# Staging the plain attention heads token by token through DRAM, with two direct batches and partial first sums

## The chip, the cores and the metric

The kernel runs on one core of one Trainium2 chip. The metric is the device time of one execution in microseconds (us), as the median of several runs. The hardware profiler also took one execution; its trace has the start and length of every instruction, and "the span" is the time from its first instruction to its last.

## The reference, cut to what matters

Eight batches of eight heads with 576 tokens and a head dimension of 64 go through windowed causal attention. Heads 0 to 3 ("plain") see the last 32 tokens; heads 4 to 7 ("dilated") see every fourth of the last 128. The result, 4608 tokens by 512, goes through an MLP with 2048 inner columns.

```python
mask_plain = (rel >= 0) & (rel < window)
mask_dil = (rel >= 0) & (rel < window * dilation) & (rel % dilation == 0)
...
x = np.ascontiguousarray(attn_out.transpose(0, 2, 1, 3)).reshape(B * S, H * D)
...
h = x @ w_in
g = h * (1.0 / (1.0 + np.exp(-beta * h)))
return (g @ w_out).astype(np.float32)
```

Inputs and output are fp32; the kernel multiplies in bf16 and sums in fp32 in PSUM.

## The kernel before

The MLP goes over nine tiles of 512 tokens. A tile has 16 h slots, one for each 128 of the 2048 inner columns, of four matmuls each (`slot_h`, L824: one for each k-tile of 128 of the 512 columns of x), and 16 o slots of four matmuls (`block`, `block_cols`, L856: four blocks of 128 tokens, four slots each). After an h slot ACT takes a tanh (L831) and DVE makes the gate (L836, g). After four o slots ACT or DVE scales the block into osb (L873, L875), and SP or ACT stores it (L881). The k-tiles 0 and 1 of x hold the plain heads, 2 and 3 the dilated ones. Of tile 0, the first four h slots are cut into 288 and 224 columns (SPLIT), since a batch's x comes in two halves of 288 tokens.

Attention of a batch is worked between the slots of the MLP, about two tiles ahead. Its steps have names in the lists FIRST (batches 0 to 2) and LATER (the rest). S2 and S3 are scores of dilated heads (L644), as pairs of matmuls on 64 rows each; T is the scores of the last 16 tokens of each dilated class (L618, from dkt and qt); S00 and so on are scores of the plain heads in blocks of 96 queries. ACT takes the exponential (L586), DVE or POOL multiplies by a mask (L590), V.. and U multiply by the values (L740, L725, L755), DVE normalizes (L604, L605) into xsp, xdm and xdt, and X.. brings the result into xT: by PE transposes in batches 0 and 1 (L778, L780, L796), by DRAM in the others (`back_dma`: writes x<-xsp, x<-xdm, x<-xdt on SP, then the crossbar, a transposing DMA, from DRAM to xT at L490).

K and Q come in two ways. Batches 0 to 2 (DIRECT) are loaded into st by `direct_qk` and transposed on TensorE (KD and QD for dilated heads, L427; KP and QP for plain ones, L434, as 64x64 pairs), then copied into dk, dq, kT and qT. Batches 3 to 7 are cast from fp32 to bf16 into DRAM (s) on POOL's DMA queue (`cast`, `load`, issued at L368), in rows of 1024 elements, and brought by four crossbars on SP (`crossbar`, L417) into dk and dq, and into raw for the plain heads. There, even and odd tokens lie on the two halves of the partitions, so `spread` copies them into kz, which is padded with zeros to 128 rows, and qd (L218, on DVE or POOL). The plain scores of these batches are matmuls over all 128 rows (L703, with masks maske), those of batches 0 to 2 pairs over 64 rows (L678, with masks maskn). A cast from batch 4 on waits for the crossbars of the batch before.

v is loaded three times by POOL's queue: vp (plain, 128-byte rows in bf16), vt (the tails), and vd16 or st, copied into vd. The late masks and the zeros of kz are made on POOL in one step, t_late (L317 to L362).

The order of all instructions on every engine is written out by a planner (`Plan`). Each step has engines with costs, dependencies and a due time vt, given in tiles. `run` takes, again and again, the step that can start first, and among those that can start at nearly the same time (NEAR) the one that is due first. PSUM is eight banks; CAPS says how many may be held for each kind of use. Where nothing is ready before 80 us of the plan, it puts in filler matmuls on zeros (L968). The engines then work strictly in this order, each waiting on semaphores. POOL issues the loads and casts (queue q0), SP the crossbars, write-backs and stores (queue q1).

Of the kernel before, what the change touches and what calls it, by code (L numbers as in the profile page):

```python
# [9 lines left out]
BF16 = mybir.dt.bfloat16  # L10
ACT = mybir.ActivationFunctionType
ALU = mybir.AluOpType
# [10 lines left out]
class Op:  # L23
    def __init__(self, engs, fn, deps, vt, acquire, group, dma, lat):
# [10 lines left out]
class Plan:  # L35
# [3 lines left out]
    CAPS = {"h": 3, "o": 2, "z": 4, "a": 8, "s": 5}  # L39
# [6 lines left out]
    def op(self, engs, fn, deps=(), vt=0.0, acquire=None, group=None, dma=0, lat=None):  # L46
        acquire = acquire if acquire is None or isinstance(acquire, list) else [acquire]
        o = Op(engs, fn, deps, vt, acquire, group or acquire, dma, lat)
        self.ops.append(o)
        return o  # L50

    def run(self, filler=None, filler_until=0.0):
# [13 lines left out]
        ends = []  # L66

# [19 lines left out]
        while n_left:  # L87
            best = None
            near = {}
            for o in avail:  # L90
                base = o.ready
                at = {e: max([free[e], base] + [t for x, t in o.group.read.items() if x != e]
                             if o.group is not None and e != "PE" else [free[e], base]) for e, d in o.engs}
                fin = min(at[e] + d for e, d in o.engs)
# [18 lines left out]
            if filler is not None and s <= filler_until and free["PE"] + 300 < s:  # L113
# [5 lines left out]
                free["PE"] = now + 225  # L119
                continue  # L120
# [6 lines left out]
            o.fn(e)  # L127
            free[e] = s + d
            o.start, o.end = s, s + d + self.LAT[e]
# [27 lines left out]
FIRST = "KD0 QD0 KD1 QD1 KP0 QP0 KP1 QP1 S2 S3 T S00 S10 V20 V21 V30 V31 U V00 V10 X2 X3 X00 X10 S01 S11 V01 V11 X01 X11"  # L157
LATER = "S2 S3 T V20 V21 V30 V31 U S00 S10 S01 S11 X2 X3 V00 V10 X00 X10 S02 S12 V01 V11 X01 X11"
# [3 lines left out]
def kernel(  # L162
# [34 lines left out]
    DIRECT = 3  # L197
    ADDED = 1
    BY_DMA = 2
    SPLIT = 4  # L200
# [16 lines left out]
    def copy(e, out, in_):  # L217
# [10 lines left out]
    mask_e = {n: const([P, 2, 2, 2, QT // 2], BF16, f"maske_{n}") for n in ("FP", "PP")}  # L228
# [14 lines left out]
    ptt = const([P, 2, 288], BF16, "ptt")  # L243
    ptt_own = ptt[0:2 * KTL][:, :, 0:256].rearrange(
        "p c (h s) -> p c h s", h=4)[:, :, :, 0:2 * UT]
# [9 lines left out]
    raw = const([P, 2, 4, S // 2], BF16, "raw")  # L255
    vd16 = raw[:].rearrange("p z h m -> p (z h m)")[:, 0:1024].rearrange("p (h T d) -> p h T d", h=4, T=C)
    vd16_of = [vd16] * DIRECT + [st[b % 2][:, 0:1024].rearrange(
        "p (h T d) -> p h T d", h=4, T=C) for b in range(DIRECT, B)]
    kT = [const([P, WIN + S], BF16, f"kT{x}") for x in range(2)]
    kz = const([P, 4, WIN + S], BF16, "kz")  # L260
    qd = const([P, 4, 2, S // 2], BF16, "qd")
    qT = qd[:].rearrange("p (x f) e m -> p x (f e m)", x=2)[:, :, 0:S]
# [27 lines left out]
    def t_fill1(e):  # L290
        for x in range(2):
            nc.vector.memset(kT[x][:, 0:WIN], 0.0)
# [709 lines left out]
```

The softmax here doesn't subtract the row's maximum and nothing guards it: scores larger than these inputs give would overflow.

## Time and profile before

| what | us |
|---|---|
| median of 3 runs | 311.29 (310.63 to 311.44) |
| the profiled execution | 311.41 |
| its span | 309.7 |
| TensorE busy (PE) | 297.0 |
| VectorE busy (DVE) | 199.1 |
| ScalarE busy (ACT) | 171.3 |
| GpSimd busy (POOL) | 108.6 |
| first h slot begins | 20.07 |

The granted TensorE clock was 0.998. PE is matmuls, PEld the loads of weights beside them. A line of the timeline has the start, the busy time, the engine, the line of the kernel, the operation, its output and input by their names, the tile and the count; in brackets stands the idle time before it and what ended that. Ends of matmuls are modelled, so a group's own cost is read from the start of the next. A digit in the slices is a share of busy time in tenths of one fortieth of the span.

### The profile page before, as it was taken

What the parts mean: (1) busy time and instruction counts of PE and PEld (TensorE: products, weight loads), DVE (VectorE), ACT (ScalarE), POOL (GpSimd) and SP (SyncE); (2) the same over time, 40 slices, a digit from 0 to 9 for tenths busy, and PEclk for the clock granted to TensorE, in tenths of its full rate; (3) what the DMA queues carried; (4) which work ended last, traced back from release to release, by engine and by line L of the source; (5) the groups of instructions that cost most, each with busy time, mean ns of one, the idle gap of its engine ahead of it and who ended that gap; (6) DMA issues with size and microseconds to landing.
All of it is one profiled execution on the core that took longest, in us unless ns stands there. A gap on an engine that the chain in (4) does not pass through costs nothing.

```text
span 309.7 us, 6029 instructions
## 1 busy us (share of the span) xinstructions
PE 297.0 (96%) x2270; PEld 153.6 (50%) x2307; DVE 199.1 (64%) x421; ACT 171.3 (55%) x302; POOL 108.6 (35%) x150
## 2 busy tenths in 40 slices
PE   7899999999999999999999999999999999999994
PEld 5565546454454445444455454445544444444452
DVE  4687868888958777775896878677853443434300
ACT  2668845866448445753775547555754544554311
POOL 8989754537170146414823651154000000000000
PEclk9999999999999999999999999999999999999999
DMA  6999999999689982999999759997024100001112
GB/s 100 168 210 207 206 187 208 230 155 174 155 163 178 191 151 83 180 160 181 188 206 181 197 117 177 129 224 163 18 64 112 44 34 34 36 34 60 42 70 69
DMA packets 93561, 42.48 MB, mean 137 GB/s; under 512 B 71052, under 2 KB 88220, under 8 KB 93212
## 3 DMA queue, kind: packets, MB, share of 16 engines
q0 software_dynamic: 42336, 19.66, 50.3%
q1 hardware_dynamic: 51052, 22.37, 35.0%
q8 instruction: 18, 0.29, 0.4%
q14 instruction: 11, 0.09, 0.1%
q10 hardware_dynamic: 144, 0.07, 0.1%
HBM read 39.32 MB, written 18.87 MB: 188 GB/s over the span
## 4 chain that ended last, share of the span: by engine, by line
PE 82%; POOL 6%; DMA 6%; DVE 2%; issue 2%; ACT 0%; POOLq 0%; ACTq 0%; DVEq 0%
PE bank L856 38%; PE bank L824 35%; DMA raw<-in_v_dram 3%; DMA vp<-in_v_dram 3%; PE bank L703 2%; PE bank L755 2%; POOL st L368 1%; PE bank L740 1%; PE bank L644 1%; PE bank L725 1%; POOL kz L362 1%; DVE qt L218 1%; DVE g L836 1%; PE bank L434 0%; PE bank L618 0%
## 5 line engine op out<-in xcount | busy, mean ns | idle before, releaser
L831 ACT ACTIVATE tnh<-bank,beta_half 128x512 bf16<-128x512 f32 (+2 forms) x148 | 100.1, 677 | 81.8 <-PE bank L824 73.6
L836 DVE SCALAR_TENSOR_TENSOR g<-tnh,bank 128x512 bf16<-128x512 bf16 (+2 forms) x148 | 98.7, 670 | 69.2 <-ACT tnh L831 68.1
L824 PE MATMUL bank<-xT,w_in_bf 128*128 128x512 bf16 (+2 forms) x576 | 139.8, 373 | 1.3 <-DVE xT L218 0.3
L856 PE MATMUL bank<-w_out_bf,g 128*128 128x512 bf16 (+1 forms) x571 | 137.7, 373 | 1.8 <-DVE g L836 0.5
L856 PEld LDWEIGHTS <-g 128*128 128x128 bf16 x592 | 55.4, 98 | 58.6 <-issue 0.8
L824 PEld LDWEIGHTS <-w_in_bf 128*128 128x128 bf16 x592 | 55.1, 98 | 58.2 <-issue 0.8
L873 ACT ACTIVATE osb<-bank 128x512 f32<-128x512 f32 (+2 forms) x36 | 21.0, 582 | 28.4 <-PE bank L856 23.5
L586 ACT ACTIVATE pt<-bank 128x384 bf16<-128x384 f32 (+1 forms) x54 | 22.0, 455 | 6.4 <-PE bank L703 3.5
L586 ACT ACTIVATE ptd<-bank 128x512 bf16<-128x512 f32 x32 | 17.0, 601 | 10.3 <-PE bank L644 10.3
L605 DVE TENSOR_TENSOR xsp<-bank,rcp 96x384 bf16<-96x384 f32 x32 | 17.7, 554 | 1.1
L604 DVE RECIPROCAL rcp<-bank 128x4 f32<-128x4 f32 (+2 forms) x72 | 12.8, 177 | 5.5 <-PE bank L755 2.8
L218 POOL COPY kz<-raw 64x1152 bf16<-64x1152 bf16 x6 | 9.4, 1566 | 18.4 <-DMA raw<-s 18.3
L218 POOL COPY vd<-st 128x1024 bf16<-128x1024 bf16 x4 | 4.1, 1037 | 30.9 <-DMA st<-in_v_dram 30.9
L590 DVE TENSOR_TENSOR ptd<-ptd,mask_d 128x512 bf16<-128x512 bf16 x24 | 13.0, 575 | 2.8 <-ACT ptd L586 2.5
L605 DVE TENSOR_TENSOR xdm<-bank,rcp 128x256 bf16<-128x256 f32 x32 | 13.6, 424 | 1.1
L590 POOL TENSOR_TENSOR pt<-pt,maske_FP 128x384 bf16<-128x384 bf16 x7 | 6.3, 912 | 20.4 <-ACT pt L586 12.4
L368 POOL DMA_DIRECT2D vp<-in_v_dram x9 | 12.0, 1338 | 2.6 <-DMA vp<-in_v_dram 2.6
L755 PEld LDWEIGHTS <-pt 128*128 128x128 bf16 x192 | 9.2, 97 | 6.5 <-DVE pt L590 0.6
L755 PE MATMUL bank<-vp,pt 128*128 128x65 bf16 x192 | 10.6, 193 | 0.9 <-DVE pt L590 0.5
L368 POOL DMA_DIRECT2D vt<-in_v_dram x16 | 11.0, 694 | 0.0
L875 DVE TENSOR_SCALAR osb<-bank 128x512 f32<-128x512 f32 (+1 forms) x2 | 1.0, 486 | 13.7 <-ACT osb L873 13.7
L218 DVE COPY qd<-raw 64x1152 bf16<-64x1152 bf16 x14 | 8.9, 634 | 0.9 <-DMA raw<-s 0.8
(125 smaller groups left out, 223.4 us busy)
## 6 DMA issues: line engine op xcount, KB each, us to landing
out_dram<-osb SPq DMA_DIRECT2D x35, 256.0 KB, 2.0
s<-in_k_dram POOLq DMA_DIRECT2D x5, 576.0 KB, 7.6
s<-in_q_dram POOLq DMA_DIRECT2D x5, 576.0 KB, 10.2
vp<-in_v_dram POOLq DMA_DIRECT2D x7, 384.0 KB, 14.8
w_out_bf<-in_moe_w_out_dram POOLq DMA_DIRECT2D x2, 1024.0 KB, 16.3
st<-in_k_dram POOLq DMA_DIRECT2D x6, 288.0 KB, 13.3
st<-in_q_dram POOLq DMA_DIRECT2D x6, 288.0 KB, 13.5
x<-xsp SPq DMA_DIRECT2D x20, 72.0 KB, 2.3
```

Source lines behind the costliest of these rows:

```text
L218: (nc.scalar.copy if e == "ACT" else E[e].tensor_copy)(out=out, in_=in_)
L368: {"POOL": nc.gpsimd, "SP": nc.sync}[queue].dma_start(out=out, in_=in_)
L586: nc.scalar.activation(out=w(), in_=sc(), func=ACT.Exp, scale=SCALE)
L590: E[e].tensor_tensor(out=w(), in0=w(), in1=m(), op=ALU.mult)
L604: nc.vector.reciprocal(out=r, in_=p[..., D])
L605: nc.vector.tensor_tensor(out=dst, in0=p[..., 0:D], in1=r.unsqueeze(len(p.shape) - 1).to_broadcast(list(p.shape[:-1]) + [D]), op=ALU.mult)
L755: nc.tensor.matmul(pv[:, a, h2, :], lhsT=pt[x][:, (3 * j + a) * 2 + h2], rhs=vp[kv][:, (2 * x + h2) * NI + 3 * j + a, 0:D + 1], start=True ...
L824: nc.tensor.matmul(bank(g)[:, 0:n], lhsT=w_in_bf[:, kt, fb * P:(fb + 1) * P], rhs=xT[:, kt, xo:xo + n], start=(kt == 0), stop=(kt == NKT - 1))
L831: nc.scalar.activation(out=th[:, 0:n], in_=bank(g)[:, 0:n], func=ACT.Tanh, scale=beta_half[:, fb:fb + 1])
L836: nc.vector.scalar_tensor_tensor(out=g_t[t % 2][:, fb, c0:c0 + n], in0=th[:, 0:n], scalar=1.0, in1=bank(g)[:, 0:n], op0=ALU.add, op1=ALU.mult)
L856: nc.tensor.matmul(bank(g)[:, lo:hi], lhsT=g_t[t % 2][:, fb, tb * P:(tb + 1) * P], rhs=w_out_bf[:, fb, lo:hi], start=(fb == 0), stop=(fb = ...
L873: nc.scalar.mul(out=ob[:, cols], in_=bank(g)[:, cols], mul=0.5)
```

## The change

- DIRECT is 2: batch 2 goes through DRAM and the crossbar too.
- A cast takes four heads instead of eight. That of the dilated heads keeps rows of 1024 elements. That of the plain heads writes each token's four heads side by side, in pieces of 64 elements, so that the crossbar brings them straight into kT and qT, which are now double. raw, kz, qd, the copies between them, and maske go. Casts wait no more for the crossbars of the batch before.
- All plain scores are pairs over 64 rows, in blocks of three (288 columns), with masks maskn; the masks are planned singly and earlier. S02 and S12 go from LATER.
- In batch 0, T and U come after everything else, with own tail transposes Y2 and Y3; its vt loads come later, and its vp in three pieces, so that the values of heads 0 and 1 wait only for two of them. Batch 1 has an order of its own, NEXT.
- The first four h slots are no longer cut by tokens: k-tiles 2 and 3 are summed over all 512 columns first, then 0 and 1 over 288 and 224 (APART, PSUM kind "p").
- The writes x<-xsp and x<-xdt are one DMA each per half. Readiness of xT is kept by k-tile.
- The last block's columns are cut 256, 128, 128, each with later due times and one copy of its own, and all stores are on SP.
- The planner counts a cost for each change between full and half rows on TensorE, keeps copies that only touch SBUF on DVE and POOL apart, and has other costs for masks.

```diff
-    CAPS = {"h": 3, "o": 2, "z": 4, "a": 8, "s": 5}
+    CAPS = {"h": 3, "p": 4, "o": 2, "z": 4, "a": 8, "s": 5}
+    SWITCH = 95
...
+                if o.sbuf:
+                    at = {e: max(t, port["DVE" if e == "POOL" else "POOL"]) for e, t in at.items()}
...
+            if e == "PE" and o.halves != halves:
+                halves = o.halves
+                d += self.SWITCH
...
-FIRST = "KD0 QD0 KD1 QD1 KP0 QP0 KP1 QP1 S2 S3 T S00 S10 V20 V21 V30 V31 U V00 V10 X2 X3 X00 X10 S01 S11 V01 V11 X01 X11"
-LATER = "S2 S3 T V20 V21 V30 V31 U S00 S10 S01 S11 X2 X3 V00 V10 X00 X10 S02 S12 V01 V11 X01 X11"
+FIRST = "KD0 QD0 KD1 QD1 KP0 QP0 KP1 QP1 S2 S3 S00 S10 V20 V21 V30 V31 V00 V10 X2 X3 X00 X10 S01 S11 V01 V11 X01 X11 T U Y2 Y3"
+NEXT = "KD0 QD0 KD1 QD1 KP0 QP0 KP1 QP1 S2 S3 T S00 S10 V20 V21 V30 V31 U V00 V10 X2 X3 X00 X10 S01 S11 V01 V11 X01 X11 Y2 Y3"
+LATER = "S2 S3 T V20 V21 V30 V31 U S00 S10 X2 X3 V00 V10 X00 X10 S01 S11 V01 V11 X01 X11"
...
-    DIRECT = 3
+    DIRECT = 2
     ADDED = 1
     BY_DMA = 2
-    SPLIT = 4
+    APART = 4
...
-    raw = const([P, 2, 4, S // 2], BF16, "raw")
-    vd16 = raw[:].rearrange("p z h m -> p (z h m)")[:, 0:1024].rearrange("p (h T d) -> p h T d", h=4, T=C)
-    vd16_of = [vd16] * DIRECT + [st[b % 2][:, 0:1024].rearrange(
+    vd16 = const([P, 4, C, D], BF16, "vd16")
+    vd16_of = [vd16[:]] * DIRECT + [st[b % 2][:, 0:1024].rearrange(
         "p (h T d) -> p h T d", h=4, T=C) for b in range(DIRECT, B)]
-    kT = [const([P, WIN + S], BF16, f"kT{x}") for x in range(2)]
-    kz = const([P, 4, WIN + S], BF16, "kz")
-    qd = const([P, 4, 2, S // 2], BF16, "qd")
-    qT = qd[:].rearrange("p (x f) e m -> p x (f e m)", x=2)[:, :, 0:S]
+    kT = [const([P, 2, WIN + S], BF16, f"kT{i}") for i in range(2)]
+    qT = [const([P, 2, S], BF16, f"qT{i}") for i in range(2)]
...
+        half = 2 * NI
+        return [load("POOL", (vp[0][WIN:P, 0:half, 0:D], plain_v(0, WIN, 0)[:, 0:half]), deps, vt, 288, .25),
+                load("POOL", (vp[0][0:WIN, 1:half, 0:D], plain_v(0, 0, 1)[:, 0:half - 1]), deps, vt, 92, .25),
+                load("POOL", (vp[0][:, half:, 0:D], plain_v(0, 0, half)), deps, vt, 384, .27)]
...
+            out.append(load("POOL", (vt_[b % 2][:, c, :, 0:D], src), list(tdeps), vt + (1.245 if b == 0 else .02 if b < DIRECT else 0) + .001 + .001 * c, 96, .2))
...
-    def cast(b, z, deps, vt):
-        dst = scratch[b, z] = dram_pool.tile([2, S * 4 * D], BF16, name=f"s{b}_{z}")
-        src = (k, q)[z][b].rearrange("(x h) s d -> x (h s d)", x=2)
-        return load("POOL", (dst[:].rearrange("x (a e) -> (x a) e", e=1024),
-                             src.rearrange("x (a e) -> (x a) e", e=1024)), deps, vt, 1152, .38)
+    def cast(b, z, h0, deps, vt):
+        dst = scratch[b, z, h0] = dram_pool.tile([S * 4 * D], BF16, name=f"s{b}_{z}_{h0}")
+        src = (k, q)[z][b, h0:h0 + 4]
+        if h0:
+            args = (dst[:].rearrange("(a e) -> a e", e=1024), src.rearrange("h s d -> (h s d)").rearrange("(a e) -> a e", e=1024))
+        else:
+            args = (dst[:].rearrange("(s h d) -> s h d", h=4, d=D), src.rearrange("h s d -> s h d"))
+        return load("POOL", args, deps, vt, 576, .38 if h0 else .25, 500 if h0 else 3000)
     def crossbar(b, z, h0, deps, vt):
-        flat = scratch[b, z][h0 // 4]
+        kv = b % 2
         if h0:
-            dst = (dk, dq)[z][b % 2][:].rearrange("p r h t -> p r (h t)")
-            src = flat.rearrange("(a e) -> a e", e=C * D)
+            dst = (dk, dq)[z][kv][:].rearrange("p r h t -> p r (h t)")
         else:
-            dst = raw[:, z].rearrange("p h m -> p (h m)").unsqueeze(1)
-            src = flat.rearrange("(a e) -> a e", e=P)
+            dst = qT[kv][:] if z else kT[kv][:, :, WIN:]
+        src = scratch[b, z, h0][:].rearrange("(a e) -> a e", e=C * D)
...
-            for e_ in range(2):
-                def spread(e, e_=e_):
-                    rows = slice(64 * e_, 64 * e_ + 64)
-                    dst = kz[rows, :, WIN:].rearrange("p h (m e) -> p h m e", e=2)[:, :, :, e_]
-                    copy(e, dst, raw[rows, 0])
...
-            ready["P"] = ops
+            ready = {"D": [ld["x", 0, 4], ld["x", 1, 4]], "P": [ld["x", 0, 0], ld["x", 1, 0], fill1]}
...
-                        nc.tensor.matmul(
-                            sc[:, a, h2 * QT:h2 * QT + QT],
-                            lhsT=kz[:, 2 * x + h2, i * QT:i * QT + P],
-                            rhs=qd[:, 2 * x + h2, :, i * QT // 2:(i + 1) * QT // 2],
-                            start=True, stop=True)
...
+                        nc.tensor.matmul(
+                            bank(gs[h])[:, a * QT:(a + 1) * QT], lhsT=kT[kv][rows, x, i * QT:i * QT + P],
+                            rhs=qT[kv][rows, x, i * QT:(i + 1) * QT], start=b >= ADDED, stop=b >= ADDED or a == 2)
...
-        for e_ in range(2 if b >= DIRECT else 0):
-            out.append(plan.op(
-                [("SP", 500)], lambda e, e_=e_: nc.sync.dma_start(
-                    out=plain[e_], in_=xsp[j][e_ * QT // 2:(e_ + 1) * QT // 2].rearrange("p a x h d -> p a (x h d)")),
-                [vdone[0, j], vdone[1, j]], vt_of[f"X1{j}"], dma=600, lat=2000))
+        out = [plan.op(
+            [("SP", 500)], lambda e: nc.sync.dma_start(
+                out=rows[:, 0:HD // 2].rearrange("(i m) c -> m i c", m=QT),
+                in_=xsp[j][:].rearrange("p a x h d -> p a (x h d)")),
+            [vdone[0, j], vdone[1, j]], vt_of[f"X1{j}"], dma=1200, lat=2000)]
...
-            for c in range(C):
-                dil.append(plan.op(
-                    [("SP", 500)], lambda e, c=c: nc.sync.dma_start(
-                        out=right[t1 - t0:, c], in_=xdt[(c % 2 * 2 + c // 2) * UT:(c % 2 * 2 + c // 2 + 1) * UT].rearrange("p x h d -> p (x h d)")),
-                    [vdone["U"]], vt_of["X11"], dma=150, lat=2000))
+            dil.append(plan.op(
+                [("SP", 500)], lambda e: nc.sync.dma_start(
+                    out=right[t1 - t0:].rearrange("u c e -> c u e"), in_=xdt[:].rearrange("p x h d -> p (x h d)")),
+                [vdone["U"]], vt_of["X11"], dma=300, lat=2000))
...
+        parts = [((2, 3), 0, n), ((0, 1), 0, S // 2), ((0, 1), S // 2, n)] if apart else [((0, 1, 2, 3), 0, n)]
...
-        for lo, hi in ((0, HD // 2), (HD // 2, HD)) if last_one else ((0, HD),):
-            block_cols(t, tb, vts, lo, hi, (lo, (lo + hi) // 2, hi) if lo else (lo, hi))
+        cuts = (0, HD // 2, 3 * HD // 4, HD) if last_one else (0, HD)
+        for i, (lo, hi) in enumerate(zip(cuts, cuts[1:])):
+            block_cols(t, tb, [x + i for x in vts], lo, hi)
...
-            behind = [ld[b - 1]["x", z, h0] for z in range(2) for h0 in (0, 4)] if b > DIRECT else []
-            cs = [cast(b, z, gop[b - 2, 0] + behind, b - 2 + .01 * z) for z in range(2)]
             for n, (z, h0) in enumerate(((0, 4), (1, 4), (0, 0), (1, 0))):
-                key = ((("dk", "dq")[z], b % 2, 0), (("dk", "dq")[z], b % 2, 1)) if h0 else (("raw", z),)
-                extra = war("vd16") if not h0 else []
-                ld[b]["x", z, h0] = crossbar(b, z, h0, [cs[z]] + war(*key) + extra, b - 2 + .01 * n)
+                c = cast(b, z, h0, gop[b - 2, 0], b - 2 + .01 * n)
+                key = [(((("dk", "dq") if h0 else ("kT", "qT"))[z]), b % 2, i) for i in range(2)]
+                ld[b]["x", z, h0] = crossbar(b, z, h0, [c] + war(*key), b - 2 + .01 * n)
```

## The prediction

> **What bounds the kernel now.** I read the page's busy line, slices and chain of waits first, then the windows by stage, then TensorE's timeline.
>
> ```profile
> PE 297.0 (96%) x2270; PEld 153.6 (50%) x2307; DVE 199.1 (64%) x421; ACT 171.3 (55%) x302; POOL 108.6 (35%) x150
> ...
> PE   7899999999999999999999999999999999999994
> ...
> PE 82%; POOL 6%; DMA 6%; DVE 2%; issue 2%; ACT 0%; POOLq 0%; ACTq 0%; DVEq 0%
> ```
>
> ```profile
> 0.00:34.20 34.20, 29.41 (x434) 19.97 (x436) 23.23 (x67) 21.64 (x44) 31.08 (x61) 1.00 1.19 175
> 34.20:112.00 77.80, 75.67 (x651) 38.70 (x663) 61.81 (x138) 47.70 (x91) 33.44 (x41) 1.00 1.26 184
> 112.00:290.35 178.35, 177.18 (x1108) 86.79 (x1129) 113.08 (x215) 98.23 (x162) 44.13 (x49) 1.00 0.69 117
> ```
>
> The columns of the windows are length, then PE, PEld, DVE, ACT and POOL, then clock, DMA share and GB/s. TensorE is the bound: after 112 us it is busy for 177.18 of 178.35. So the time is TensorE's own work, plus its few stalls, which lie before 112 us; there the DMA share is also highest, 1.26 of 16 engines' span. Everything taken from DVE, ACT or POOL alone is worth nothing unless a stall goes with it.
>
> The prices come from starts in TensorE's timeline, since ends are modelled.
>
> ```profile
> 35.47 1.04 PE L824 MATMUL bank<-xT,w_in_bf 128*128 128x512 bf16 x4
> 36.44 0.30 PE L678 MATMUL bank<-qd,kT 64*128 64x96 bf16 x6
> 36.67 1.04 PE L824 MATMUL bank<-xT,w_in_bf 128*128 128x512 bf16 x4
> ...
> 55.08 0.47 PE L434 MATMUL bank<-ident_b,st 64*64 64x64 bf16 x18
> 55.48 1.04 PE L824 MATMUL bank<-xT,w_in_bf 128*128 128x512 bf16 x4
> 56.45 0.75 PE L434 MATMUL bank<-ident_b,st 64*64 64x64 bf16 x36
> ...
> 90.81 8.80 PE L824 MATMUL bank<-xT,w_in_bf 128*128 128x512 bf16 x39
> 99.45 0.33 PE L703 MATMUL bank<-qd,kz 128*128 128x96 bf16 x4
> 99.62 1.03 PE L824 MATMUL bank<-xT,w_in_bf 128*128 128x512 bf16 x4
> ```
>
> From 90.81 to 99.45 go ten slots of four 512-column matmuls (one record is missing): 0.864 us a slot, 216 ns a matmul. Four zero-padded scores (L703) take 99.45 to 99.62, 0.17. Six scores of 64-row pairs (L678) take 0.23, but the slot before them takes 0.97 rather than 0.864: 0.105 to change over, so 0.34 a group. The transposes of 64x64 (L434) pay the same: 55.48 to 56.45 is again 0.97.
>
> **What the skill says.** "TensorEngine Tiling (Array Packing)", Key Properties: a change of tiling mode drains TensorE. The 0.105 above agrees. "DMA: Bandwidth & Descriptors", Specifications: full rate needs transfers of at least 512 B, below which the engine reads, modifies and writes. The trace has slow 128-byte packets, but into SBUF only; no row writes 128 bytes to DRAM. Its section "Queues, rings and completion order": an engine takes turns between queues packet by packet. The trace agrees:
>
> ```profile
> q0 software_dynamic: 2956, 0.38, 236.2%
> ```
>
> ```profile
> q1 hardware_dynamic: 1544, 0.39, 102.3%
> q0 software_dynamic: 978, 0.12, 54.1%
> ```
>
> The first is 99.5 to 102 us, a load of 128-byte packets nearly alone: 1180 a us. The second is 66.5 to 70 us, the same sort beside a crossbar transpose: 280 and 440 a us. "SBUF — State Buffer", section "SBUF: two separate sides": DVE and GpSimd share a port pair that one holds for a whole instruction. The trace agrees: the qt copy pair takes 0.39 us at 8.94 and 2.11 us at 76.47, beside GpSimd's kz and qd copies.
>
> **The change part by part.**
>
> *Batch 2 by crossbar.* Its PE transposes go: L427 in groups of 0.25, 0.27 and 0.52 (starts 50.32, 51.49 and 51.88), L434 in 0.40, 0.68 and 0.40 (55.08, 56.45 before its wait, 58.10), with three changes of mode: 1.04 + 1.48 + 0.3 = 2.8 us off TensorE. They stand between slots with nothing else to do there, so all of it counts. Its dilated scores, two groups of 8, become one of 16: one change and one start-up less, -0.2. One or two start fillers go, -0.1. Its eight evacuation copies were hidden.
>
> *All plain scores in 64-row pairs.* A batch had 24 padded matmuls, 24 x 0.0425 = 1.02 us. Four groups of six cost 4 x 0.34 = 1.37. In the new order batches 4 to 7 stand so: +0.35 x 4 = 1.4; batch 3 stands as 12, 6, 6 (twelve cost 0.36 + 0.105): +0.1; batch 1 loses a joined group, +0.2, so +1.7 in all. ACT gets 64 exps of 288 in place of 24 of 288 and 30 of 384, the same elements and ten starts more: hidden, ACT being 55% busy.
>
> *Copies gone (qd, kz, their memset and masks).* 14 + 4 on DVE and 12 on POOL, nothing on TensorE by themselves. What they can give back is the stalls between 34 and 112 us. TensorE's durations summed from 34.27 give 303.43 as its end against 305.23 in the trace: 1.8 us of stall, all before 112 (0.47 at 79.35 and 0.50 at 102.24 behind DVE, 0.26 at 40.17 behind POOL). I leave the 1.8 in: the gate and mask waits come from order, which stays dense.
>
> *Start (partial first sums, later T, U and tails).* k-tiles 2 and 3 need only dilated heads, so the first MLP matmul need not wait for the plain ones: it starts at 20.07 now, and could at about 19.0, when the first quarter of w_in lands (19.04). But the next batch's loads land at 28.30, 29.72, 31.19 and 32.60, and TensorE takes each at once (28.35, 29.77, 31.25, 32.65, the last after 0.32 of idle). They are paced by POOL's queue, which the change hardly touches up to there. So of 1.0 us I take one slot: eleven done at 34.27 in place of ten, -0.86. Bounds: 0 (all paced) to -1.7 (two slots); the later tail values can cost 0.3.
>
> *Casts and crossbars.* For batches 2 to 7 each cast is split; the plain half is written token by token, 2304 packets of 128 bytes in DRAM, where before 18 KB rows went. They are issued on POOL's queue, past vd, vt and vp loads; their issue takes POOL about what the vp issue takes (1.34 us for 3072), hidden at 35% busy. The transfer isn't in the trace. Low end 1.45 us, half of a 576 KB cast that took 61.7 to 64.4 (2.9 with its start); at 1180 packets a us it is 2.0; beside crossbars, or with slow short writes, 4 to 5. I take 2.0. A gain beyond the low end is excluded, for no bytes go. The queue after 47.2 us, when the vt loads of batch 1 end, is: batch 2 dilated k and q (48.7, 50.1), plain k and q beside crossbars and vp (56.1, 61.7), vp (66.6); batch 3 dilated (68, 69.5), plain k 75.4, plain q 80 to 82.5. Batch 2 is in time (scores wanted at 70.9, landing at 64.7). Batch 3's q is wanted at 85.8. What is queued behind matters more: SP works in order, and its crossbar for q of batch 3 waits for that cast, with the write-back of batch 2's x and its xT transpose behind it. xT lands about 9.7 us after the cast (SP held 2.4 by the crossbar, 70.46 to 72.88; x<-xsp 2.3 to landing, the page's median; 3.0 to issue the two xT transposes, below; about 2 to land, an estimate from x<-xdt's 1.8 at 77.05), so at 90 to 92. In the new order TensorE has used up every output slot of tiles 0 and 1 when it comes to tile 2's first slot, at 92.0; before, six were left at 90.81. The stall is 0 to 2 us: I take +0.8. From batch 4 on casts are released far ahead, so nothing is added.
>
> ```profile
> 79.98 2.99 SPq L490 DMA_TRANSPOSE xT<-x  x2
> ```
>
> *Joined write-backs (one xsp and one xdt in place of 2 and 4), stores all on SP.* SP issues fewer; what they hide behind is MLP of the tile before. If that cover is gone it is the stall above.
>
> *Tail.* TensorE ends at 305.23; ACT's 256 columns run 304.88 to 305.26, its 128 to 305.59, and DVE's 128 only then:
>
> ```profile
> 304.88 0.71 ACT L873 ACTIVATE osb<-bank 128x256 f32<-128x256 f32 x2 [1.15 <-PE bank L856]
> ```
>
> ```profile
> 305.62 0.29 DVE L875 TENSOR_SCALAR osb<-bank 128x128 f32<-128x128 f32 x1 [13.67 <-ACT osb L873]
> ```
>
> With 256, 128 and 128 columns and their own due times only one 128 copy is left behind the last matmul: -0.3. The cut itself has the same TensorE columns.
>
> *Sum.* -2.8 - 0.2 - 0.1 + 1.7 - 0.86 = -2.3 of work; -0.3 tail; +0.8 stall: -1.8. The profiled execution took 311.41 (span 309.7, 1.71 around it), so 309.6; it lies 0.1 above the median of 311.29, so 309.5.
>
> **Rivals.** (1) *Slower: the token-wise casts.* Four stand before batch 3's q, so each us more per cast moves xT of batch 2 and q of batch 3 by 4, and the stall by nearly that. At 4 us each: 8 late, 309.5 + 7.3 = 316.8 (stall 8 in place of 0.8). It is past 312.2 from about 2.8 us a cast. For it: beside crossbars q0 moved a quarter of its lone packets. Against: half of the stretch has no crossbar. (2) *No change: the start doesn't do what it says.* The loads pace it, no slot is gained and the late tail values stall 0.3: 309.5 + 0.86 + 0.3 = 310.7. For it: the 0.32 idle at 32.65. Casts of 2.4 to 2.7 us end here too. (3) *More:* no stall and two slots: 309.5 - 0.8 - 0.86 = 307.8. For it: POOL and DVE lose copies that hold each other up. Against: xT's slack is about zero.
>
> **How the numbers follow.** About 0.3% (0.9 us) is what a measurement of this kernel tells from no change. Forecast (308.3 to 310.4, all but 0.02 of it faster) 0.46; rival 3 (faster) 0.08; rival 2 0.18; rival 1 (312.2 to 318) 0.28. So faster 0.52, same 0.20, slower 0.28. The range from 307.5 to 315.5 leaves out the worst of rival 1 and a little below, under 0.2.
>
> **What would show it.** Right: no transposes of staged rows after 35 us; groups of six at 0.34; first h near 19.0 and eleven slots at 34.3; plain casts of batch 3 landed by 82; a stall under 2 us ahead of tile 2's first slot near 92, ended by the DMA to xT; one copy after the last matmul. Wrong: that stall, or one before the plain scores of batch 2 or 3, of 4 us or more, with plain casts of over 2.8 us each; or TensorE's work not 2 us shorter.

## The result and the profile after

The changed kernel took 347.9 us (345.44 to 353.86), against 311.4 in the same comparison: 1.115 times as long, with a 95% interval of 1.109 to 1.121. The forecast was 309.5 with a range from 307.5 to 315.5. The times of this kernel, and of others below that wait much, scatter by one to six per cent, and ratios leave out runs more than 1.5% above the fastest of their kernel.

Page of the kernel after: TensorE has holes that it did not have, and its granted clock (PEclk, in tenths) falls behind most of them.

```profile
span 345.7 us, 5841 instructions
...
PE 307.7 (89%) x2216; PEld 150.7 (44%) x2216; DVE 180.9 (52%) x413; ACT 169.4 (49%) x310; POOL 93.3 (27%) x131
...
PE   8899999575998937699919999999999999999995
...
PEclk9999999958799996999978999999999999999999
...
PE 59%; DMA 33%; POOL 3%; DVE 2%; SPq 1%; issue 1%; ACT 0%; POOLq 0%; ACTq 0%; DVEq 0%
```

Before, DMA had 6% of the chain; now it has 33%. The windows by stage of the kernel after (columns as before) put all of the damage between 34 and 200 us. From 200 us on TensorE is full.

```profile
0.00:34.20 34.20, 30.86 (x431) 19.90 (x432) 21.90 (x62) 21.50 (x45) 29.19 (x58) 1.00 1.20 176
34.20:112.00 77.80, 65.56 (x499) 31.77 (x498) 42.42 (x110) 35.68 (x76) 29.71 (x37) 0.89 1.63 155
112.00:200.00 88.00, 69.14 (x441) 31.51 (x440) 47.01 (x102) 40.96 (x72) 29.92 (x35) 0.92 1.39 151
200.00:300.00 100.00, 100.00 (x622) 46.81 (x623) 57.13 (x122) 54.75 (x95) 4.49 (x5) 1.00 0.59 99
```

In the second line the DMA engines are busier than before (1.63 where 1.26 was) and move less (155 GB/s where 184 was). TensorE's waits in the kernel after, in us, times and longest:

```profile
PE bank L800 <- DMA xT<-x: 15.6, 2, 7.9
PE bank L631 <- DMA dq<-s: 9.9, 2, 6.8
PE bank L664 <- DMA qT<-s: 3.9, 2, 3.7
```

All three end with a crossbar. The two waits before 112 us (6.8 for dq, which ends at 71.61, and 3.7 for qT, which ends at 85.33) are for batch 2. SP's timeline of the kernel after, around the first of the waits, has the start and the time that a crossbar holds SP:

```profile
49.42 2.41 SPq L434 DMA_TRANSPOSE dk<-s  x1
52.51 3.21 SPq L434 DMA_TRANSPOSE dq<-s  x1
55.82 8.15 SPq L434 DMA_TRANSPOSE kT<-s  x1
64.46 13.16 SPq L434 DMA_TRANSPOSE qT<-s  x1
```

That time is not the transfer's own. SP also stood while earlier transfers of its queue had not gone. Each crossbar moves 1152 packets of 256 bytes, and these can be counted off in the packet records, here without the first and last 2%: those of kT ran from 67.75 to 77.14 us, 9.4 us, and those of qT only from 77.39 to 82.83, so that most of qT's 13.16 us of SP passed while kT's packets ran. In the kernel before, the slowest crossbar of K or Q held SP for 4.8 us:

```profile
132.78 4.80 SPq L417 DMA_TRANSPOSE raw<-s  x1
```

The loss adds up. These waits are 29.4 us. The mean clock of 0.956 over 345.7 us is 30.4 us at half clock; by the clock record 11.3 of them lie inside waits, and the other 19 at half speed cost 9.6. Together 39, where the span grew by 36.0. So what is left of the kernel became about 3 us shorter, as the prediction's -2.3 of work and -0.3 of tail said, though this is a small difference of large numbers. The half clock is a second price of four of the five waits over 3 us; the one of 3.1 us that ended at 144.00 brought none. The Trainium skill ("TensorE: Matmul & The Clock Gate", Part 1) says that an idle TensorE drops to half clock and needs a busy window of some 3.4 us to come back. The trace agrees on the way back: full clock came 3.4 to 6.1 us after TensorE went on, and the half-clock stretches last 6.8 us or 10.2 us. For the drop, the same table names an idle window of some 3.4 us too; here it came as early as 2.7 us after TensorE stopped (at 67.49, after 64.84). A slot inside a stretch takes 1.7 us where 0.864 is usual:

```profile
71.61 1.04 PE L631 MATMUL bank<-dq,dk 64*128 64x128 bf16 x16 [6.78 <-DMA dq<-s]
72.58 0.53 PE L605 MATMUL bank<-qt,dkt 128*96 128x64 bf16 x4
72.92 1.89 PE L835 MATMUL bank<-w_out_bf,g 128*128 128x512 bf16 x4
74.60 1.91 PE L800 MATMUL bank<-xT,w_in_bf 128*128 128x512 bf16 x4
```

### The profile page after: what moved, and what is told of

Its sections match the earlier page's. It is cut to its first block, busy times and chain, and to the rows that moved or that the text cites. A ratio compares the mean times of both kernels' runs of the same rounds, so it can differ in the third digit from the quotient of the medians.

```text
span 345.7 us, 5841 instructions
## 1 busy us (share of the span) xinstructions
PE 307.7 (89%) x2216; PEld 150.7 (44%) x2216; DVE 180.9 (52%) x413; ACT 169.4 (49%) x310; POOL 93.3 (27%) x131
## 4 chain that ended last, share of the span: by engine, by line
PE 59%; DMA 33%; POOL 3%; DVE 2%; SPq 1%; issue 1%; ACT 0%; POOLq 0%; ACTq 0%; DVEq 0%
PE bank L835 30%; PE bank L800 25%; DMA qT<-s 10%; DMA xT<-x 6%; DMA vp<-in_v_dram 5%; DMA s<-in_q_dram 5%; DMA x<-xsp 5%; DMA w_in_bf<-in_moe_w_in_dram 2%; PE bank L664 2%; DVE g L814 1%; PE bank L718 1%; POOL st L380 1%; POOL vp L380 1%; SPq L498 1%; PE bank L703 1%
## 5 line engine op out<-in xcount | busy, mean ns | idle before, releaser
L800 PE MATMUL bank<-xT,w_in_bf 128*128 128x512 bf16 (+1 forms) x584 | 146.3, 385 | 16.7 <-DMA xT<-x 15.6
L809 ACT ACTIVATE tnh<-bank,beta_half 128x512 bf16<-128x512 f32 x144 | 98.3, 688 | 107.2 <-PE bank L800 104.0
L814 DVE SCALAR_TENSOR_TENSOR g<-tnh,bank 128x512 bf16<-128x512 bf16 x144 | 97.9, 685 | 95.5 <-ACT tnh L809 94.9
L835 PE MATMUL bank<-w_out_bf,g 128*128 128x512 bf16 (+2 forms) x608 | 147.5, 375 | 0.0
L850 ACT ACTIVATE osb<-bank 128x512 f32<-128x512 f32 (+1 forms) x35 | 20.6, 588 | 26.1 <-PE bank L835 22.7
L572 ACT ACTIVATE pt<-bank 128x288 bf16<-128x288 f32 x64 | 22.6, 413 | 13.0 <-PE bank L664 12.3
L576 POOL TENSOR_TENSOR pt<-pt,maskn_PP 128x288 bf16<-128x288 bf16 x13 | 9.6, 859 | 39.7 <-ACT pt L572 39.7
L591 DVE RECIPROCAL rcp<-bank 128x4 f32<-128x4 f32 (+2 forms) x72 | 12.9, 179 | 9.8 <-PE bank L718 4.8
L380 POOL DMA_DIRECT2D s<-in_q_dram x12 | 14.4, 1200 | 9.5 <-DMA s<-in_q_dram 8.8
L380 POOL DMA_DIRECT2D s<-in_k_dram x12 | 13.5, 1128 | 7.2 <-DMA w_out_bf<-in_moe_w_out_dram 3.9
L664 PE MATMUL bank<-qT,kT 64*128 64x96 bf16 x192 | 9.8, 214 | 3.9 <-DMA qT<-s 3.9
## 6 DMA issues: line engine op xcount, KB each, us to landing
s<-in_k_dram POOLq DMA_DIRECT2D x12, 288.0 KB, 13.2
x<-xsp SPq DMA_DIRECT2D x12, 144.0 KB
```

The source lines that it names most:

```text
L380: {"POOL": nc.gpsimd, "SP": nc.sync}[queue].dma_start(out=out, in_=in_)
L572: nc.scalar.activation(out=w(), in_=sc(), func=ACT.Exp, scale=SCALE)
L576: E[e].tensor_tensor(out=w(), in0=w(), in1=m(), op=ALU.mult)
L591: nc.vector.reciprocal(out=r, in_=p[..., D])
L664: nc.tensor.matmul(bank(gs[h])[:, a * QT:(a + 1) * QT], lhsT=kT[kv][rows, x, i * QT:i * QT + P], rhs=qT[kv][rows, x, i * QT:(i + 1) * QT], ...
L800: nc.tensor.matmul(bank(g)[:, a:z], lhsT=w_in_bf[:, kt, fb * P:(fb + 1) * P], rhs=xT[:, kt, xo + a:xo + z], start=(i == 0 and kt == kts[0] ...
```

## The experiments

Eighteen kernels, in the order in which they ran. A word on the first ones: "wait" in their expectations, and in the account of the kernel before, is what I thought a dependency in the planner to be. It is not. It only moves the step in the written order. The chip waits only where data calls for it, and POOL runs up to eight transfers ahead (at 60 us in the kernel after, eight were issued and had not landed). I saw this only after the thirteenth run.

**First round: which packets?** The packet records showed the 18 KB packets of dilated casts running while crossbars stood still, so I took these for the cause.

Dilated casts behind the crossbars of the batch before:

```diff
-                c = cast(b, z, h0, gop[b - 2, 0], b - 2 + .01 * n)
+                c = cast(b, z, h0, gop[b - 2, 0] + (behind if h0 else []), b - 2 + .01 * n)
```

> The dilated casts of batches 3 to 7 wait again for the four crossbars of the batch before; all else is as changed. Theory 'long packets': a dilated cast goes out as 32 packets of 18 KB for each batch, each holds its DMA engine for 1.38 us, and a crossbar beside it stands still for that time on all engines. Then the DMA waits of TensorE (29 us in the changed kernel) nearly go: 307 to 313 us. Rival 'short writes': the token-wise casts themselves are slow beside crossbars (9.4 us and 8.9 us landed). Then nothing of that goes: 340 us or more.

335.3 us (ratio 1.078, 1.073 to 1.083): between the two expectations.

Packets of 2 KB in place of 18 KB:

```diff
-            args = (dst[:].rearrange("(a e) -> a e", e=1024), src...rearrange("(a e) -> a e", e=1024))
+            rows = lambda t: t.rearrange("(x a e) -> a x e", x=2, e=1024)
+            args = (rows(dst[:]), rows(src.rearrange("h s d -> (h s d)")))
```

> The dilated casts go out in packets of 2 KB in place of 18 KB, by taking the rows from two halves in turn; same bytes, same place, same order on all engines. Long packets: a crossbar waits at most about 0.15 us for one of them, so the DMA waits nearly go: 307 to 313 us. Short writes: unchanged, 345 us.

348.3 us (1.111, 1.105 to 1.117): nothing gained. The length of the packets is not the cause.

No token-wise writes:

```diff
-            args = (dst[:].rearrange("(s h d) -> s h d", h=4, d=D), src.rearrange("h s d -> s h d"))
+            args = (dst[:].rearrange("(a e) -> a e", e=1024), src...rearrange("(a e) -> a e", e=1024))
```

> The plain casts are written in long rows like the dilated ones in place of token by token, so that the plain heads attend with mixed-up keys and queries; same bytes, same order. Long packets: 64 of them for each batch in place of 32, so no faster: 345 to 385 us. Short writes: 308 to 315 us, since no short writes are left.

352.0 us (349.3 and 354.8): nothing gained. The short writes, which were my main worry in the prediction, are not the cause either.

The kernel before, with its casts freed:

```diff
-            cs = [cast(b, z, gop[b - 2, 0] + behind, b - 2 + .01 * z) for z in range(2)]
+            cs = [cast(b, z, gop[b - 2, 0], b - 2 + .01 * z) for z in range(2)]
```

> The kernel before, its casts no longer waiting for the crossbars of the batch before. Long packets: batches 4 to 7 have their casts beside crossbars, four batches of the kind that cost the changed kernel some 7 us each: 318 to 345 us. Short writes: it has none, so 311 us within 1 us.

312.45 us (1.002, 1.000 to 1.004): no effect that can be told. In its trace the casts of batch 4 still come after the crossbars of batch 3. So the line that the change took away was not what kept them apart. Both theories of this round had failed.

**Second round: how much lies side by side?**

All four casts behind the crossbars of the batch before:

```diff
-                c = cast(b, z, h0, gop[b - 2, 0], b - 2 + .01 * n)
+                c = cast(b, z, h0, gop[b - 2, 0] + behind, b - 2 + .01 * n)
```

> All four casts of a batch, plain ones too, wait for the crossbars of the batch before; all else is as changed. Theory 'pile-up': casts and loads of two batches lie in POOL's queue beside the crossbars of one, and the crossbars, with all that stands behind them on SP, are held up by the next batch's traffic. Then 308 to 318 us. Rival 'too many packets': the 27,600 more 128-byte packets are themselves what the DMA engines can't carry beside crossbars, wherever they lie. Then 328 us or more, as much as with only the dilated casts waiting (335).

326.9 us (1.049, 1.043 to 1.056), between the two again.

Besides, crossbars behind all four casts of their own batch:

```diff
+            cs = [cast(b, z, h0, gop[b - 2, 0] + behind, b - 2 + .01 * n) for n, (z, h0) in enumerate(steps4)]
...
-                ld[b]["x", z, h0] = crossbar(b, z, h0, [c] + war(*key), b - 2 + .01 * n)
+                ld[b]["x", z, h0] = crossbar(b, z, h0, cs + war(*key), b - 2 + .01 * n)
```

> As the run before, and a batch's crossbars start only when all four of its casts have landed, so no cast of any batch lies beside a crossbar; vp and vt still do. Pile-up: 308 to 318 us, no better than the run before by more than 3. If casts beside crossbars of the same batch are a price of their own: at least 5 us less than the run before. Too many packets: 325 us or more.

316.45 us (1.015, 1.008 to 1.021), 10.5 less than the run before. That is the second expectation: casts of a batch cost something beside its own crossbars too. SP's timeline of this kernel has the four crossbars of batch 3 in a quiet stretch:

```profile
86.80 1.32 SPq L434 DMA_TRANSPOSE dk<-s  x1
88.22 1.26 SPq L434 DMA_TRANSPOSE dq<-s  x1
89.58 1.36 SPq L434 DMA_TRANSPOSE kT<-s  x1
91.04 1.56 SPq L434 DMA_TRANSPOSE qT<-s  x1
```

5.5 us for the four, which held SP for 13.7 in the kernel after. The four of batch 2 held it for 26.9 there, and still for 15.4 here.

Three direct batches, all else as changed:

```diff
-    DIRECT = 2
+    DIRECT = 3
```

> Three direct batches as before the change, all else as changed, so that batch 2 has no casts and crossbars. Pile-up: batches 2 and 3 no longer collide at 50 to 95 us, where the changed kernel waits 10.5 us for dq and qT and runs some time at half clock; later batches still collide: 322 to 338 us. Too many packets: about the fifth of the loss, 338 to 344 us.

324.7 us (1.042, 1.036 to 1.049). It lies in the range of the pile-up theory. A good half of the loss goes with the one batch more in the queue at the start.

The kernel before with two idle token-wise casts for each batch:

```diff
+            for z in range(2):
+                spare = dram_pool.tile([S * 4 * D], BF16, name=f"e{b}_{z}")
+                load("POOL", (spare[:].rearrange("(s h d) -> s h d", h=4, d=D),
+                              (k, q)[z][b, 0:4].rearrange("h s d -> s h d")), [cs[z]], ...)
```

> The kernel before, and for each of batches 3 to 7 two token-wise casts more (k and q of the plain heads, into DRAM that nobody reads), behind its own casts in POOL's queue. Same number of short writes for each batch as in the changed kernel, on top of the old casts. Pile-up: the casts are spaced by their waits as before, 311 to 315 us. Too many packets: the crossbars and vp of the same batch come late, 320 us or more.

318.1 us (1.022, 1.018 to 1.025), between the two expectations. Nobody reads these casts, so what they cost is the room they take beside others; TensorE waits 3.2 us for xT.

**Third round: can the separation be kept?**

The separated kernel (316.45) with three direct batches:

```diff
-    DIRECT = 2
+    DIRECT = 3
```

> Casts and crossbars kept apart both ways, and three direct batches. Kept apart with two direct batches took 316.5, of which the trace gives 3.4 us to waits for dq and xT and some 4.5 us to half clock after them; without these 308.5, and the transposes of batch 2 add 2.8: 309.5 to 312 us. If staging token by token has another price in later batches, 314 us or more.

333.4 us (1.066, 1.061 to 1.071): over 20 us above the first expectation. TensorE waits 12.9 us for xT in it; the crossbars of x had not been separated from anything.

The separated kernel with another issue cost of a plain cast:

```diff
-        return load("POOL", args, deps, vt, 576, .38 if h0 else .25, 500 if h0 else 3000)
+        return load("POOL", args, deps, vt, 576, .38 if h0 else .25, 500 if h0 else 1700)
```

> Casts and crossbars kept apart both ways with two direct batches, and the planner told that issuing a token-wise cast takes POOL 1.7 us, as the trace has it, and not 3.0. SP then takes the crossbars of batch 3 ahead of one write-back of batch 2 for which it had waited. Pile-up: the wait for dq at 92 us and the half clock behind it go, 308 to 312 us. If that wait comes from the casts themselves, 314 to 318 us.

328.5 us (1.054, 1.051 to 1.057): a miss too. The wait for dq at 92 us is gone, but now the crossbars of batch 4 fall beside the v loads of batches 4 and 5, and hold SP for 15.2 us.

The separated kernel with long rows in the plain casts, by the edit of the third run:

> Casts and crossbars kept apart both ways, and the plain casts in long rows in place of token by token, so that the plain heads attend with mixed-up keys and queries. If the short writes cost nothing of their own once apart: 316.5 us within 2. If they still do: 309 to 313 us.

315.0 us (1.010, 1.007 to 1.013). Against 316.45 this is 1.5 us for 12 token-wise casts once they lie apart, with intervals that overlap.

Crossbars behind their own casts only, the next batch's casts free:

```diff
-            cs = [cast(b, z, h0, gop[b - 2, 0] + behind, b - 2 + .01 * n) for n, (z, h0) in enumerate(steps4)]
+            cs = [cast(b, z, h0, gop[b - 2, 0], b - 2 + .01 * n) for n, (z, h0) in enumerate(steps4)]
```

> Only the second half of the separation: a batch's crossbars wait for all of its own casts, but the next batch's casts go out freely, as in the changed kernel. Pile-up by the next batch: 328 us or more, little of the loss returns. If it was the batch's own casts: 316 to 324 us.

353.9 us (1.113, 1.108 to 1.118; the runs behind this ratio took 346.6 to 351.5): nothing returns, as the first expectation had it. It does not single out the next batch's traffic, though. In its trace batch 2's own plain q cast landed at 59.93, and its vp at 75.90, while its crossbars held SP from 50.84 to 76.15: the plan kept nothing apart there.

**Fourth round: the rest of the change, and real waits.**

The separated kernel, and the loads of v behind the crossbars of their batch:

```diff
+            xs = [ld[b]["x", z, h0] for z in range(2) for h0 in (0, 4)]
...
-            ld[b]["vp"] = direct_vp(b, gop[b - 2, 2] + war(("vp", b % 2)), b - 2 + .03)
+            ld[b]["vp"] = direct_vp(b, xs + war(("vp", b % 2)), b - 2 + .03)
```

> Kept apart both ways with two direct batches, and the loads of v of batches 2 to 7 (vp, vt and the vd source) go out only when the four crossbars of their own batch have landed. Then nothing of POOL's queue but the next casts lies beside crossbars of K and Q, whatever the order falls out to be. Pile-up: these crossbars hold SP for 1.3 to 2 us each, and the time is 308 to 314 us. Rival 'phase alone' (kept apart with two direct batches was lucky, and waits arise elsewhere): v now lands late for its values, 316 us or more.

333.1 us (1.071, 1.067 to 1.075): a miss of the first expectation, and in the range of the rival. But POOL's and SP's timelines of this kernel show that the loads and casts were not held back at all: casts of batch 3 go out at 49.54, though they stood "behind" crossbars of batch 2 that start at 53.74.

```profile
49.54 0.53 POOL L380 DMA_DIRECT2D s<-in_k_dram  x1
50.23 0.51 POOL L380 DMA_DIRECT2D s<-in_q_dram  x1 [0.16 <-issue]
```

```profile
53.74 4.66 SPq L434 DMA_TRANSPOSE dk<-s  x1
58.51 6.39 SPq L434 DMA_TRANSPOSE dq<-s  x1
```

The old staging (cast, crossbar, raw, kz, qd, their scores and three direct batches, as in the kernel before) inside the changed kernel, in short:

```diff
-                c = cast(b, z, h0, gop[b - 2, 0], b - 2 + .01 * n)
+            cs = [cast(b, z, gop[b - 2, 0] + behind, b - 2 + .01 * z) for z in range(2)]
...
-            dst = qT[kv][:] if z else kT[kv][:, :, WIN:]
+            dst = raw[:, z].rearrange("p h m -> p (h m)").unsqueeze(1)
```

> K and Q of batches 3 to 7 staged as before the change (casts in long rows behind the crossbars of the batch before, kz and qd, three direct batches), and the rest as changed: the start with partial first sums, the orders of batches 0 and 1, the joined writes where the layout allows, the tail. If the staging is the whole loss: no DMA wait over 2 us; the start gives 0.86 and the tail 0.3 to 0.9, so 309.5 to 311 us. If the rest has a part in the loss: 313 us or more.

311.1 us (0.998, 0.997 to 1.000), and no DMA wait of TensorE over 0.8 us. The staging of K and Q, with its two direct batches, is the whole loss. The start, the orders of batches 0 and 1 and the tail cost nothing.

Real waits: one DRAM buffer for each cast, shared by all batches, so that a cast has to wait until the crossbar of the batch before has read it. The plan also keeps the separation both ways, and takes 1.7 us for the issue of a plain cast, here and in the kernels that follow:

```diff
+    ORDER = ((1, 0), (0, 0), (1, 4), (0, 4))
+    slots = [dram_pool.tile([S * 4 * D], BF16, name=f"s{i}") for i in range(4)]
...
-        dst = scratch[b, z, h0] = dram_pool.tile([S * 4 * D], BF16, name=f"s{b}_{z}_{h0}")
+        dst = scratch[b, z, h0] = slots[ORDER.index((z, h0))]
```

> The separation by real waits. So far a dependency given to the planner only moved a step in the order; on the chip an engine waits only for data, and POOL ran up to eight transfers ahead. Here all batches share one DRAM buffer for each of the four casts, so a cast must wait until the crossbar of the batch before has read it, and the casts go plain q, plain k, dilated q, dilated k, so that the first crossbar (dilated k) waits for the last cast. The loads of v still lie beside the crossbars. Pile-up: 309 to 318 us. If the crossbars are slow for another reason: 325 us or more.

325.7 us (1.045, 1.041 to 1.049), in the range of the second expectation. But 11 of the 24 crossbars of K and Q still have POOL's queue beside them, and what runs there is the loads of v alone.

Besides, the loads of v between the first and the second cast:

```diff
-            ld[b]["vp"] = direct_vp(b, gop[b - 2, 2] + war(("vp", b % 2)), b - 2 + .03)
+            go = gop[b - 2, 0] + behind
...
+            ld[b]["vp"] = direct_vp(b, go + war(("vp", b % 2)), b - 2 + .0016)
```

> As the run before, and the loads of v stand in POOL's queue between the first and the second cast of their batch, so that they have landed before its crossbars start. Nothing of POOL's queue lies beside a crossbar of K or Q of batches 3 to 7. Pile-up: these crossbars hold SP for about 1.4 us each, 308 to 314 us, and no slower than the run before. If what is left comes from late casts, 318 us or more.

320.0 us (1.027, 1.023 to 1.031), the second expectation. POOL's timeline of this kernel now shows the wait, for the last crossbar of batch 2:

```profile
68.69 1.62 POOL L380 DMA_DIRECT2D s<-in_q_dram  x1 [4.47 <-DMA qT<-s]
```

Every crossbar of K and Q is quick, but batch 3 comes too late behind batch 2. TensorE's waits in this kernel, longest first:

```profile
PE bank L633 <- DMA dq<-s: 8.2, 1, 8.2
PE bank L802 <- DMA xT<-x: 1.3, 1, 1.3
```

The same with three direct batches:

```diff
-    DIRECT = 2
+    DIRECT = 3
```

> Real waits, loads of v among the casts, and three direct batches, so that the first staged batch has no other ahead of it. The run with two direct batches had only one large wait left, for dq of batch 3 (8.2 us, and half clock for some time behind it; without both, and the small waits at that place, about 306 us). Three direct batches take that wait away and bring back 2.8 us of transposes: 308 to 311 us if the pile-up was the cause; 314 us or more if the serial chain of casts and crossbars is now too long in later batches as well.

310.83 us (310.24 to 312.03) against 311.64: 0.998, 0.997 to 0.999. All 36 us are gone, with token-wise casts, direct layout and row pairs as changed, but with three direct batches. It takes both: three direct batches alone gave 324.7, real waits with two 320.0. Page, TensorE's longest DMA wait and SP's timeline of this kernel:

```profile
PE 300.2 (97%) x2312; PEld 150.4 (49%) x2312; DVE 183.3 (59%) x407; ACT 167.2 (54%) x310; POOL 102.9 (33%) x145
```

```profile
PE bank L446 <- DMA st<-in_k_dram: 1.1, 1, 1.1
```

```profile
73.77 1.35 SPq L436 DMA_TRANSPOSE dk<-s  x1
75.23 1.63 SPq L436 DMA_TRANSPOSE dq<-s  x1
76.97 1.51 SPq L436 DMA_TRANSPOSE kT<-s  x1
78.57 2.06 SPq L436 DMA_TRANSPOSE qT<-s  x1
```

Two direct batches again, batch 3's casts ahead of its loads, and its crossbars ahead of those of batch 2's x:

```diff
+            if b == DIRECT + 1:
+                for _, _, _, o in xcopy[-2:]:
+                    o.deps += [ld[b]["x", z, h0] for z in range(2) for h0 in (0, 4)]
...
+            ld[b]["vp"] = direct_vp(b, go + war(("vp", b % 2)), b - 2 + (.0016 if b > 3 else .016))
```

> Real waits with two direct batches as before, loads of v among the casts from batch 4 on; of batch 3 the casts go first, and SP takes the crossbars of batch 3 ahead of those of x of batch 2. The wait for dq of batch 3 shrinks from 8.2 to 0 to 3 us, and that for x of batch 2 grows by up to 3: 308 to 315 us.

317.6 us (1.019, 1.017 to 1.022), a miss, though the waits for dq and xT are gone. TensorE now waits between 69 and 102 us for results of DVE and ACT, nine times and at most 1.5 us, and its mean clock is 0.982.

**All runs side by side.** For each crossbar of K or Q I took from SP's timeline how long it holds SP, and from the DMA records how many packets of POOL's queue begin in that time. "Busy" is over 100 a us, a line drawn after the runs. It counts packets, so traffic in long packets looks smaller than it is, and it leaves out the crossbars of x.

| kernel | us | crossbars: SP held, sum | quiet: count, mean | busy: count, mean |
|---|---|---|---|---|
| before | 311.3 | 49.3 | 10, 2.0 | 10, 2.9 |
| after | 347.9 | 88.7 | 9, 2.0 | 15, 4.7 |
| dilated casts behind | 335.3 | 79.3 | 7, 1.5 | 17, 4.1 |
| all casts behind | 326.9 | 72.7 | 8, 1.7 | 16, 3.7 |
| kept apart in the plan | 316.5 | 45.4 | 18, 1.5 | 6, 3.1 |
| kept apart, three direct | 333.4 | 46.4 | 15, 2.1 | 5, 2.9 |
| kept apart, planned sooner | 328.5 | 61.2 | 12, 1.4 | 12, 3.7 |
| real waits | 325.7 | 57.0 | 13, 1.6 | 11, 3.3 |
| real waits, loads too | 320.0 | 35.4 | 24, 1.5 | 0 |
| real waits, loads, three direct | 310.8 | 29.9 | 20, 1.5 | 0 |

Where the separation held, a quiet crossbar held SP for about 1.5 us; a busy one held it for two to three times that on average. Single ones were held for up to 13.2 us in the kernel after and 21.0 in the one without token-wise writes. By the packets themselves, the 7 crossbars of K and Q in the kernel after with next to nothing of POOL's queue beside them took 1.3 us on average, the other 17 took 4.3 on average and 9.4 at most; in the last kernel of the table all 20 ran alone, at 1.5. In the kernel with real waits the busy ones had only loads of v beside them, which write into SBUF, so neither casts nor writes to DRAM are needed for it. The sum alone does not set the time: kept apart with three direct batches it is as small as with two, and that kernel took 17 us longer, by its waits for xT.

## Why the prediction was wrong

The step that failed is "Casts and crossbars": it put the stall at +0.8 us, and the waits came to 29.4. "I take 2.0" for a token-wise cast fitted one place: batch 2's first plain cast landed at 51.88, 1.87 us behind the one before it (50.01), while no packet of a crossbar moved. I laid all transfers one after another at such prices, with a crossbar at 2.4 us from one row of the kernel before. Beside each other both were slower. The busy crossbars held SP not for 2.4 but for 4.7 us on average. The next three plain casts landed 9.4, 4.5 and 3.9 us behind the transfer before them, batch 2's vp 13.9 us behind where 4.9 were laid, and batch 3's plain q at 94.14 where 82.5 was the latest. I had looked at what a crossbar does to POOL's queue (280 packets a us in place of 1180), and not at what POOL's queue does to a crossbar. The kernel before would have told: counted as in the table above, its busy crossbars already took 2.9, and one 4.8.

"From batch 4 on casts are released far ahead, so nothing is added" was the wrong way round. That casts go out far ahead is what brings them beside the crossbars of the batch before; 19 of the 29 us of waits come after 112 us (7.9 at 131.95, 3.1 at 144.0, 7.7 at 180.17), where I had expected none:

```profile
131.95 1.87 PE L800 MATMUL bank<-xT,w_in_bf 128*128 128x512 bf16 x4 [7.88 <-DMA xT<-x]
144.00 0.62 PE L631 MATMUL bank<-dq,dk 64*128 64x128 bf16 x16 [3.12 <-DMA dq<-s]
180.17 4.19 PE L800 MATMUL bank<-xT,w_in_bf 128*128 128x512 bf16 x11 [7.71 <-DMA xT<-x]
```

Holding these casts back in the plan alone gave back 21 us (326.9).

The slower rival had the right sign and half of the mechanism. Casts did slow down beside crossbars, to about the 4 us that it named and more (8 us late make 316.7 there, not 316.8). But it put this on the token-wise form, and it left the crossbars at their lone price. With no token-wise cast at all the kernel took 352.0; with token-wise casts in all five staged batches, and their crossbars undisturbed, 310.8. The place was wrong for both. No wait for xT fell near 92 us. The first two waits are for dq and qT of batch 2, of which I had said "Batch 2 is in time". That batch is the one that the change put into the queue, and three direct batches alone gave back 23 of 36 us.

I had no term for the clock. Most of the long waits for DMA cost their length and then some time at half speed: 9.6 us here.

The other steps held. The first MLP slot started at 18.74 (forecast 19.0), and by 34.0 eleven slots were done (forecast eleven at 34.3). Of batch 2 no transposes were left. Six row pairs cost what they had cost. The waits and the clock taken off, the rest is 3 us shorter, where -2.6 was said. But not all of this arrives as time: the old staging with the new start and tail gave 0.2% (311.1), at the edge of what can be told, where 1.2 us were forecast.

What stays open: why a crossbar slows down so much. One picture from the packet records of the kernel after (start, queue, bytes, duration, end in us):

```
62.29 q0 18432 1.38 63.66
62.46 q1 256   1.39 63.85
62.47 q0 128   1.39 63.86
62.49 q1 256   1.39 63.88
62.51 q1 256   1.38 63.89
```

Some thirty packets of both queues start within 0.05 us, stand for 1.4 us, and end together, just behind one long packet. That looks as if a crossbar's packets go in step, and stop for the slowest. But with 2 KB packets the time was the same (348.3), so this is argued and not shown. Open too is whether two direct batches can be had without any stall: no version without it was found.

## What to carry to other kernels

Price a transfer by the company it will have: look for the slowest row of its kind in the trace and at what ran beside it, and ask which transfers an earlier release will bring together. Crossbars ran fastest here with POOL's queue empty; give them a stretch of their own, by a wait that the data enforces, since a dependency in a planner orders and doesn't hold. And keep a term for the clock wherever TensorE stands: half clock followed most of the long waits here, and once a row of short ones.

## What the runs showed of the hardware

- The packets of a crossbar of 288 KB took 1.3 to 1.5 us on average alone, and 4.3 on average and up to 9.4 beside POOL's queue (kernel after). Casts and loads beside them slowed down too. Between 34 and 112 us the DMA engines were recorded as busier than before (1.63 against 1.26) while they moved less (155 against 184 GB/s).
- A token-wise cast, 2304 writes of 128 bytes from DRAM to DRAM, landed 1.87 us behind the transfer before it in the kernel after, and the same bytes in long rows 1.39 us (50.01 behind 48.62). The Trainium skill ("DMA: Bandwidth & Descriptors", Specifications) has full rate only from 512 bytes on, and these two intervals agree in direction; the price is small beside that of the crossbars' company. With both queues otherwise empty (real waits, loads too) the packets of such a cast took 3.3 us from first to last.
- A wait of TensorE of 2.1 us (kept apart in the plan, at 91.9 us) was followed by 10.2 us at half clock, so a short wait can cost more behind it than in it. In the last of the eighteen kernels half clock began at 97.05 us, for 10.2 us, with no wait over 1.5 us anywhere before; in the 6.8 us ahead of it TensorE was busy for 4.7.
